# One head of A, not four of B, as the last unit of a decode attention kernel, with a new column-form end

## The chip, the cores and the metric

The kernel runs on one core of one Trainium2 chip. The metric is the device time of one execution in microseconds (us), the median of several runs. The profile covers one run of each kernel; its span is about 2 us shorter than the time measured around it.

## The reference

Two independent attention blocks with one query token each. Per block there are 32 heads of 128 elements, bf16 throughout. A attends to all 16,384 keys of its cache, B only to the last 4,096 keys of its own. The two output rows of 512 stand side by side.

```python
q = (x @ wq).reshape(B, Sq, Hq, Dh).transpose(0, 2, 1, 3)
k, v = k_cache, v_cache                   # block B: only the last W = 4096 keys
scores = einsum("bhqd,bhkd->bhqk", q, k) * Dh ** -0.5
p = softmax(scores)
o = einsum("bhqk,bhkd->bhqd", p, v)
out = o.transpose(0, 2, 1, 3).reshape(B, Sq, Hq * Dh) @ wo
# result: concatenate([out_A, out_B], axis=-1)
```

So the work is almost all reading: each key and each value is used once.

## The kernel before

The kernel works in units of 4 MB of K and 4 MB of V: one head of A, or four heads of B whose keys are shared out over the partitions. After four units of A comes one of B; the order ends with A28, A29, A30, A31, B28-31. Each unit has two chunks of 64 keys per partition. For a chunk, DVE multiplies K by q (`prod`), adds the two halves (`half`), and PE sums the rest with eight matmuls against the identity (`red`); DVE and ACT make the exponentials; PE does p.v later, two chunks behind (`waiting`).

```python
for c, ch in enumerate(chunks):
    ...
    _mult(nc, cx, ch)                      # DVE: prod = K * q
    if prev is not None:
        _softmax(nc, cx, prev)             # DVE reduce, ACT exp (4 exps for a chunk of B)
        waiting.append(prev)
    fin_pe()
    _add(nc, cx, ch)                       # DVE: half
    fin_dve()
    _red(nc, cx, ch)                       # PE: q.k, 8 matmuls
    if len(waiting) > 1:
        pv(waiting.pop(0))                 # PE: p.v, needs V
    prev = ch

_softmax(nc, cx, prev)                     # ---- the end
end = prev.unit.group
fin_pe()                                   # fold of A's last group
fin_dve()                                  # its row (orow)
_late_sum_before(nc, cx, stB)              # partial row of B: copy by ACT, into PSUM
_late_sums(nc, cx, end)                    # sums of exps, bank f again
fin_pe()                                   # columns of A
fin_dve()
pv(waiting.pop(0))                         # p.v of B, first chunk
fin_pe()                                   # A's output row
_pv(nc, cx, prev, 0, (U - LATE) // 4)      # p.v of B, first half of the last chunk
_late_fold(nc, cx, end)                    # waits for acc_sb
_late_pv(nc, cx, prev, end)                # 32 keys, straight into columns
_late_out(nc, cx, end)                     # oc, output matmuls, copy, store
```

A group's normal finish is fold, row, columns, cast and output matmuls. Only the last group of the program ends in the "late" column form: its last 32 keys per partition are multiplied with V as the stationary operand, so the result stands as a column already. An instruction that waited held up the one behind it on PE: in the timeline below p.v of A31 waits 4.54 us for its V, and the reduction behind it starts 1.88 us after its input is ready.

The last V is loaded in pieces (64, 32, then, after the last part of `wo`, 16 and 16 keys). One piece is one issue for a head of A and four for four heads of B.

The softmax here doesn't subtract the row's maximum and nothing guards it: scores larger than these inputs give would overflow.

## Time and profile before

| | before |
|---|---|
| time, median (range) of 3 runs | 835.23 us (834.71 to 835.35) |
| span of the profiled run | 832.8 us |
| moved by DMA | 352.7 MB, mean 424 GB/s |
| DVE, PE, ACT busy | 70%, 49%, 8% |

These are lines of the profile's page: the span, then 40 equal slices of the span (DMA busy in tenths, and GB/s), then the chain of work that ended last, by engine.

```profile
span 832.8 us, 6118 instructions
...
DMA  9999999999999999999999999999999999999995
GB/s 383 441 435 427 414 442 427 428 432 434 438 430 429 429 428 427 431 431 433 429 439 426 429 428 430 432 430 429 433 434 432 429 430 432 428 429 433 427 427 197
...
DMA 68%; DVE 19%; issue 10%; PE 2%; SPq 1%; ACT 0%; DVEq 0%; ACTq 0%
```

The DMA engines are busy in all slices but the last, and the chain is 68% DMA. The body is bound by reading. A change that reads the same bytes finds most of its room in the last slice, some 20 us.

This is the timeline of that end (start in us, duration, engine, line, operation, `out<-in`; in brackets the idle time of the engine just ahead of it and what ended it).

```profile
811.49 2.28 DVE L189 TENSOR_TENSOR half<-prod 128x4096 bf16<-128x4096 bf16 x1
...
813.84 1.89 PE L248 MATMUL acc<-vt,pA 128*16 128x512 bf16 x16 [4.54 <-DMA vt<-in_A_v_cache_dram]
...
815.65 3.31 PE L202 MATMUL red<-half,ident 128*128 128x512 bf16 x8
...
820.68 1.04 PE L348 MATMUL f_ps<-acc_sb,sel 128*4 128x128 f32 x8 [0.68 <-ACT acc_sb L259]
...
822.82 0.39 PE L307 MATMUL out<-late_part,ones_f 1*1 1x128 f32 x8 [1.10 <-ACT late_part L302]
...
826.99 1.05 PE L278 MATMUL f_ps<-sel,acc_sb 128*128 128x4 f32 x8 [0.76 <-ACT acc_sb L259]
...
828.89 0.16 DVE L319 TENSOR_TENSOR oc<-f_ps,late_recip 128x4 bf16<-128x4 f32 x1 [4.69 <-PE f_ps L290]
...
829.75 0.27 ACT L332 CAST late_row<-out 128x128 bf16<-128x128 f32 x1 [2.81 <-PE out L325]
830.04 0.61 SPq L333 DMA_DIRECT2D out_dram<-late_row  x1
```

The reduction of the last chunk (L202 at 815.65) could have started at 813.77 (811.49 + 2.28), when DVE finished its input, the last half-sum (L189). On PE it stands behind p.v of A31 (813.84), which had waited for its V.

The windows show, per stretch: busy time of PE, PEld, DVE, ACT, POOL, then the TensorE clock (1.00 is full), the DMA share and GB/s.

```profile
core 0: us, PE busy (x) PEld busy (x) DVE busy (x) ACT busy (x) POOL busy (x), PEclk, DMA share, GB/s
...
817.00:818.00 1.00, 1.00 (x4) 0.36 (x3) 0.00 (x0) 0.00 (x0) 0.00 (x0) 0.50 0.96 348
...
821.00:822.00 1.00, 0.72 (x7) 0.35 (x4) 0.22 (x2) 1.00 (x7) 0.00 (x0) 1.00 0.90 323
...
824.00:825.00 1.00, 1.00 (x18) 0.39 (x17) 0.16 (x1) 0.00 (x0) 0.00 (x0) 1.00 0.33 111
```

Traffic falls below its 430 GB/s in this end and stops at about 825 us.

### The profile page before, as it was taken

Reading aid. Unit: us, or ns where it says so; the run is one execution under the profiler, and the core shown is the slowest. Engines: PE = TensorE matmul, PEld = TensorE weight load, DVE = VectorE, ACT = ScalarE, POOL = GpSimd, SP = SyncE. Lnnn points to the kernel's source line nnn. Section 1 sums busy time; section 2 is a strip of 40 time slices with the busy share of each in tenths; the row PEclk is TensorE's granted clock in tenths of the full one; section 3 lists DMA queues with packets and bytes.
Section 4 is the critical chain, followed back from the end, with each engine's and each line's share of the span. In section 5 each row is a group of like instructions: output and inputs, shape, how many; then the busy total and the mean of one; then the engine's idle time right before and its main releaser. Section 6 shows DMA issues by size and latency. Waiting matters only on the chain.

```text
span 832.8 us, 6118 instructions
## 1 busy us (share of the span) xinstructions
PE 410.6 (49%) x2524; PEld 141.4 (17%) x2524; DVE 585.0 (70%) x299; ACT 68.3 (8%) x301; POOL 2.9 (0%) x16
## 2 busy tenths in 40 slices
PE   3356445443555534654455443564544444554356
PEld 1112111111111111211111111121111111121113
DVE  2892666777777766777777766666677776777791
ACT  2000011000110001000020000100011000110002
POOL 1000000000000000000000000000000000000000
PEclk9778667776676666766677766677678776677767
DMA  9999999999999999999999999999999999999995
GB/s 383 441 435 427 414 442 427 428 432 434 438 430 429 429 428 427 431 431 433 429 439 426 429 428 430 432 430 429 433 434 432 429 430 432 428 429 433 427 427 197
DMA packets 16198, 352.71 MB, mean 424 GB/s; under 512 B 2730, under 2 KB 3243, under 8 KB 5419
## 3 DMA queue, kind: packets, MB, share of 16 engines
q1 hardware_dynamic: 15882, 352.33, 98.8%
q8 instruction: 19, 0.31, 0.2%
q14 instruction: 9, 0.07, 0.0%
q10 hardware_dynamic: 288, 0.00, 0.0%
HBM read 352.32 MB, written 0.00 MB: 423 GB/s over the span
## 4 chain that ended last, share of the span: by engine, by line
DMA 68%; DVE 19%; issue 10%; PE 2%; SPq 1%; ACT 0%; DVEq 0%; ACTq 0%
DMA kt<-in_A_k_cache_dram 55%; DVE prod L177 12%; DMA kt<-in_B_k_cache_dram 9%; DVE half L189 6%; DMA vt<-in_A_v_cache_dram 4%; DVE sc L219 2%; PE red L202 1%; SPq L170 1%; PE acc L248 1%; ACT p_sb L226 0%; ACT acc_sb L259 0%; PE f_ps L278 0%; PE outA L389 0%; PE f_ps L290 0%; PE out L325 0%
## 5 line engine op out<-in xcount | busy, mean ns | idle before, releaser
L202 PE MATMUL red<-half,ident 128*128 128x512 bf16 x640 | 255.4, 571 | 379.6 <-DVE half L189 379.6
L177 DVE TENSOR_TENSOR prod<-kt,qallA 128x8192 bf16<-128x8192 bf16 x64 | 283.2, 4425 | 168.0 <-DMA kt<-in_A_k_cache_dram 167.4
L189 DVE TENSOR_TENSOR half<-prod 128x4096 bf16<-128x4096 bf16 x80 | 182.5, 2281 | 0.0
L202 PEld LDWEIGHTS <-ident 128*128 128x128 bf16 x640 | 82.4, 129 | 527.0 <-issue 500.8
L177 DVE TENSOR_TENSOR prod<-kt,qallB 128x8192 bf16<-128x8192 bf16 x16 | 70.8, 4425 | 46.7 <-DMA kt<-in_B_k_cache_dram 46.4
L248 PE MATMUL acc<-vt,pA 128*16 128x512 bf16 x1024 | 87.7, 476 | 17.2 <-DMA vt<-in_A_v_cache_dram 17.1
L226 ACT ACTIVATE pA<-sc 128x64 bf16<-128x64 f32 x64 | 16.4, 256 | 520.8 <-DVE sc L219 520.8
L219 DVE TENSOR_REDUCE sc<-red 128x64 f32<-128x512 f32 x80 | 54.7, 684 | 5.3 <-PE red L202 5.3
L248 PEld LDWEIGHTS <-pA 128*16 128x16 bf16 x1024 | 23.3, 98 | 87.0 <-issue 79.5
L226 ACT ACTIVATE p_sb<-sc,off 128x64 bf16<-128x64 f32 x64 | 21.5, 337 | 98.5 <-DVE sc L219 98.5
L248 PE MATMUL acc<-vt,p_sb 128*16 128x512 bf16 x248 | 21.4, 467 | 0.0
L348 PE MATMUL f_ps<-acc_sb,sel 128*4 128x128 f32 x120 | 15.5, 272 | 5.4 <-ACT acc_sb L259 5.4
L259 ACT COPY acc_sb<-acc 128x512 f32<-128x512 f32 x16 | 9.4, 585 | 85.6 <-PE acc L248 85.6
L124 PE MATMUL q_ps<-wq_t,xbA 128*128 128x512 bf16 x32 | 8.7, 439 | 13.1 <-DMA wq_t<-in_A_wq_dram 13.1
L226 ACT ACTIVATION_READ_ACCUMULATOR p_sb<-sc,off 128x1 f32 x64 | 12.0, 187 | 0.0
L226 ACT ACTIVATION_READ_ACCUMULATOR pA<-sc 128x1 f32 x64 | 11.9, 186 | 0.0
L348 PEld LDWEIGHTS f_ps<-acc_sb,sel 128*4 128x4 f32 x120 | 9.3, 86 | 8.2 <-ACT acc_sb L259 6.2
L248 PEld LDWEIGHTS <-p_sb 128*16 128x16 bf16 x248 | 5.6, 99 | 17.1 <-issue 15.6
L389 PE MATMUL outA<-wo_t,oc 128*1 128x512 bf16 x32 | 8.2, 379 | 0.0
L124 PE MATMUL q_ps<-wq_t,xbB 128*128 128x512 bf16 x32 | 7.2, 378 | 1.7 <-DMA wq_t<-in_B_wq_dram 1.1
L389 PE MATMUL outB<-wo_t,oc 128*1 128x512 bf16 x28 | 7.7, 402 | 0.0
L96 DVE COPY xbB<-xTB 128x32 bf16<-128x32 bf16 x16 | 1.5, 197 | 8.2 <-DMA xTB<-in_B_x_dram 8.2
(44 smaller groups left out, 58.7 us busy)
## 6 DMA issues: line engine op xcount, KB each, us to landing
kt<-in_A_k_cache_dram SPq DMA_DIRECT2D x32, 4096.0 KB, 27.2
vt<-in_A_v_cache_dram SPq DMA_DIRECT2D x31, 4096.0 KB, 31.1
kt<-in_B_k_cache_dram SPq DMA_DIRECT2D x32, 1024.0 KB, 22.3
vt<-in_B_v_cache_dram SPq DMA_DIRECT2D x28, 1024.0 KB, 28.1
wq_t<-in_A_wq_dram SPq DMA_DIRECT2D x1, 4096.0 KB, 12.3
wq_t<-in_B_wq_dram SPq DMA_DIRECT2D x1, 4096.0 KB, 23.9
wo_t<-in_A_wo_dram SPq DMA_DIRECT2D x4, 1024.0 KB, 29.2
vt<-in_A_v_cache_dram SPq DMA_DIRECT2D x2, 2048.0 KB, 24.7
```

Source lines behind the costliest of these rows:

```text
L96: cx.o(nc.vector.tensor_copy(st.xb[:, c, g, :].rearrange("p (i r) -> p r i", r=R)[:, g, :], xT[:, c : c + 1].broadcast_to([P, P // R]),))
L124: cx.o(nc.tensor.matmul(q_ps[:, :], lhsT=st.xb[:, c, g, :], rhs=w[:, g, j * (512 // DH) : (j + 1) * (512 // DH), :], start=(g == 0 and c = ...
L170: cx.o(nc.sync.dma_start(out=t[g:P:n, k : k + w, :], in_=src[:, k : k + w, :]))
L177: cx.o(nc.vector.tensor_tensor(out=ch.prod[:, :, :], in0=u.kt[:, ch.k0 : ch.k0 + U, :], in1=q.rearrange("p (o d) -> p o d", o=1).broadcast ...
L189: cx.o(nc.vector.tensor_tensor(out=ch.half[:, :, :], in0=ch.prod[:, :, 0 : DH // 2], in1=ch.prod[:, :, DH // 2 : DH], op=ALU.add,))
L202: cx.o(nc.tensor.matmul(ch.red[:, :, :], lhsT=cx.ident[:, :], rhs=ch.half[:, :, b * W : (b + 1) * W], start=(b == 0), stop=(b == nb - 1),))
L219: cx.o(nc.vector.tensor_reduce(out=sc[:, :], in_=ch.red[:, :, :], axis=AX.X, op=ALU.add))
L226: cx.o(nc.scalar.activation(out=ch.p[:, :, g, :], in_=sc[:, :].rearrange("p (t e) -> p t e", e=4), func=ACT.Exp, scale=SCALE, bias=0.0 if ...
L248: cx.o(nc.tensor.matmul(gr.acc[r : r + 4 * G, :], lhsT=ch.p[:, t, :, :], rhs=u.vt[:, k : k + 4, :], start=(first and t < 4), stop=(ends an ...
L259: cx.o(nc.scalar.copy(gr.acc_sb[:, :], gr.acc[:, :]))
L348: cx.o(nc.tensor.matmul(gr.f_ps[:, 0:DH], lhsT=cx.sel[:, e, :], rhs=gr.acc_sb[:, e * DH : (e + 1) * DH], start=False, stop=(e == 3), skip_ ...
L389: cx.o(nc.tensor.matmul(st.out_ps[0:1, :], lhsT=gr.oc[:, j : j + 1], rhs=st.wo_t[i][:, g, j * st.DN : (j + 1) * st.DN], start=(gr.i == 0 a ...
```

## The change

The intent: the last unit becomes one head of A, whose V needs fewer issues and whose softmax is one exp instead of four; the last q.k does not wait behind p.v; the output row is summed in two halves in two PSUM banks, which DVE and ACT copy at the same time (0.41 and 0.36 us in its profile, the second started 0.03 us after the first). Along with this go steps: the partial row is copied when its sum is complete instead of in the end (`st.row`), the late sums get a PSUM bank of their own, and the order of the end is new. The diff, cut:

```diff
 def _late_sums(nc, cx, gr):
-    gr.f_ps = cx.psf_pool.tile([P, 2, G], F32, tag="f", name="f_ps")
+    gr.f_ps = cx.psout_pool.tile([P, 2, G], F32, tag=f"out{gr.st.name}", name="late_ps")
 ...
 def _late_sum_before(nc, cx, st):
-    part = cx.singles.tile([1, st.DN], F32, tag="late_part", name="late_part")
-    cx.o(nc.scalar.copy(part[:, :], st.out_ps[0:1, :]))
-    (one PSUM tile out4, zeroed; four matmuls of 128 columns from part)
+    (two PSUM tiles out2; two matmuls of 256 columns from st.row)
 ...
 def _late_out(nc, cx, gr):
-    row = cx.singles.tile([P, n], BF16, tag="late_row", name="late_row")
-    cx.o(nc.scalar.copy(row[:, :], st.out4[:, :]))
-    (store from four partitions)
+    row = cx.singles.tile([1, st.DN], BF16, tag="late_row", name="late_row")
+    for t, copy in enumerate((nc.vector.tensor_copy, nc.scalar.copy)):
+        cx.o(copy(row[0:1, t * n : (t + 1) * n], st.out2[t]))
+    (store from one partition)
 ...
 def _fin_out(nc, cx, gr):
-    if last and st.in_row == st.H // G:
+    if last:
+        (copies out_ps to st.row at once; the store only if the row is complete)
 ...
-        st.in_row = st.H // G - (W != SkA)
+        st.in_row = st.H // G - (W == SkA)
 ...
+    units[-2:] = units[:-3:-1]
 ...   (the last part of wo is that of A)
-        if len(waiting) > 1:
+        if len(waiting) > 1 and c < len(chunks) - 2:
             pv(waiting.pop(0))
         prev = ch
 
+    end = prev.unit.group
     _softmax(nc, cx, prev)
-    end = prev.unit.group
-    fin_pe()
-    fin_dve()
-    _late_sum_before(nc, cx, stB)
+    while waiting[0].unit is not prev.unit:
+        pv(waiting.pop(0))
+    _late_sum_before(nc, cx, end.st)
     _late_sums(nc, cx, end)
     fin_pe()
     fin_dve()
     pv(waiting.pop(0))
     fin_pe()
+    fin_dve()
     _pv(nc, cx, prev, 0, (U - LATE) // 4)
+    fin_pe()
     _late_fold(nc, cx, end)
     _late_pv(nc, cx, prev, end)
     _late_out(nc, cx, end)
```

Small tiles also move: the pool `small` goes from four buffers to two, and a pool `ends` of two takes recip, orow and oc.

More of the change, by code (lines that the diff above doesn't have):

```diff
@@ L298, in _late_sum_before @@
 def _late_sum_before(nc, cx, st):
-    part = cx.singles.tile([1, st.DN], F32, tag="late_part", name="late_part")
-    cx.o(nc.scalar.copy(part[:, :], st.out_ps[0:1, :]))
-    st.out4 = cx.red_pool.tile([P, st.DN // 4], F32, tag="red", name="out4")
-    cx.o(nc.vector.memset(st.out4[:, :], 0.0))
-    n = st.DN // 4
-    for t in range(4):
+    n = st.DN // 2
+    st.out2 = []
+    for t in range(2):
+        o = cx.red_pool.tile([P, n], F32, tag="red", name="out2")
+        st.out2.append(o[32 * t : 32 * t + 1, :])
         cx.o(nc.tensor.matmul(
-            st.out4[32 * t : 32 * t + 1, :],
+            st.out2[t],
             lhsT=cx.ones_f[0:1, 0:1],
-            rhs=part[0:1, t * n : (t + 1) * n],
+            rhs=st.row[0:1, t * n : (t + 1) * n],
             start=True, stop=False, skip_group_check=True,
@@ L316, in _late_out @@
     st = gr.st
-    n = st.DN // 4
-    gr.oc = cx.small.tile([P, G], BF16, tag="oc", name="oc")
+    n = st.DN // 2
+    gr.oc = cx.ends.tile([P, G], BF16, tag="oc", name="oc")
     cx.o(nc.vector.tensor_tensor(
@@ L322, in _late_out @@
     for j in range(G):
-        for t in range(4):
+        for t in range(2):
             f = j * st.DN + t * n
             cx.o(nc.tensor.matmul(
-                st.out4[32 * t : 32 * t + 1, :],
+                st.out2[t],
                 lhsT=gr.oc[:, j : j + 1],
@@ L330, in _late_out @@
             ))
-    row = cx.singles.tile([P, n], BF16, tag="late_row", name="late_row")
-    cx.o(nc.scalar.copy(row[:, :], st.out4[:, :]))
-    cx.o(nc.sync.dma_start(
-        out=cx.out[0, 0, st.at : st.at + st.DN].rearrange("(t f) -> t f", t=4),
-        in_=row[0:P:32, :],
-    ))
+    row = cx.singles.tile([1, st.DN], BF16, tag="late_row", name="late_row")
+    for t, copy in enumerate((nc.vector.tensor_copy, nc.scalar.copy)):
+        cx.o(copy(row[0:1, t * n : (t + 1) * n], st.out2[t]))
+    cx.o(nc.sync.dma_start(out=cx.out[0, 0:1, st.at : st.at + st.DN], in_=row[:, :]))
 def _fin_fold(nc, cx, gr):
@@ L356, in _fin_row @@
 def _fin_row(nc, cx, gr):
-    recip = cx.small.tile([G, 1], F32, tag="recip", name="recip")
+    recip = cx.ends.tile([G, 1], F32, tag="recip", name="recip")
     cx.o(nc.vector.reciprocal(recip[:, :], gr.f_ps[:, DH : DH + 1]))
-    gr.orow = cx.small.tile([G, DH], BF16, tag="orow", name="orow")
+    gr.orow = cx.ends.tile([G, DH], BF16, tag="orow", name="orow")
     cx.o(nc.scalar.activation(
@@ L379, in _fin_cast @@
 def _fin_cast(nc, cx, gr):
-    gr.oc = cx.small.tile([P, G], BF16, tag="oc", name="oc")
+    gr.oc = cx.ends.tile([P, G], BF16, tag="oc", name="oc")
     cx.o(nc.vector.tensor_copy(gr.oc[:, :], gr.oc_ps[:, :]))
@@ L397, in _fin_out @@
         cx.loads.release("wo")
-    if last and st.in_row == st.H // G:
-        row = cx.singles.tile([1, st.DN], BF16, tag=f"row{st.name}", name=f"row{st.name}")
-        cx.o(nc.scalar.copy(row[0:1, :], st.out_ps[0:1, :]))
-        cx.o(nc.sync.dma_start(out=cx.out[0, 0:1, st.at : st.at + st.DN], in_=row[0:1, :]))
+    if last:
+        done = st.in_row == st.H // G
+        st.row = cx.singles.tile(
+            [1, st.DN], BF16 if done else F32, tag=f"row{st.name}", name=f"row{st.name}"
+        )
+        cx.o(nc.scalar.copy(st.row[0:1, :], st.out_ps[0:1, :]))
+        if done:
+            cx.o(nc.sync.dma_start(
+                out=cx.out[0, 0:1, st.at : st.at + st.DN], in_=st.row[0:1, :]
+            ))
 @with_exitstack
@@ L430 @@
     cx.singles = pool("singles", 1)
-    cx.small = pool("small", 4)
+    cx.small = pool("small", 2)
+    cx.ends = pool("ends", 2)
     cx.kt_pool = pool("kt", 2)
@@ L535, in load_v, with load_wo @@
         ld.add(None if k else "vt", lambda: _load_kv(nc, cx, u, "v", k, w))
+    def load_wo(st, b, part=None):
+        ld.add(None if part else "wo", lambda: _load_wo(nc, cx, st, b, part))
     n = len(units)
     per = 2 * G
-    last_wo = stB.H // per - 1
+    last_wo = stA.H // per - 1
     ld.add("vt", lambda: _load_wq(nc, cx, stA, "vt"))
@@ L546 @@
             b = u.heads[0] // per
-            part = 0 if u.st is stB and b == last_wo else None
-            ld.add("wo", lambda st=u.st, b=b, part=part: _load_wo(nc, cx, st, b, part))
+            load_wo(u.st, b, 0 if u.st is stA and b == last_wo else None)
         if i == n - 2:
@@ L557 @@
     load_v(u, U, U - LATE)
-    ld.add(None, lambda: _load_wo(nc, cx, stB, last_wo, 1))
+    load_wo(stA, last_wo, 1)
     load_v(u, 2 * U - LATE, LATE // 2)
```

## The prediction

> **What bounds the kernel.** The span is 832.8 us, and 352.7 MB move at 424 GB/s (page, parts 1 and 3); the DMA row of the slices is 9 up to the last slice. DVE is busy 70%, PE 49%. The chain of waits is 68% DMA. So the body is DMA-bound, and keeps its bytes: only the last two units trade places (A31 and B28-31, each 4 MB of K and 4 MB of V). Nothing before about 784 us should move.
>
> **The end of before** (timeline and chain of waits). DVE finishes the last half-sum at 813.8 us. On PE the last q.k reduction stands behind the p.v of A31, which waits for its V until 813.84 and takes 1.89 us at half clock. So the reduction runs from 815.65 to 818.97. Then ACT does acc_sb 0.58, four exps (about 1.4), orow 0.34 and late_part 0.5 in series; PE does A's fold, columns and output row, B's p.v, acc_sb 0.58, fold 1.05, late p.v 0.8; oc at 828.89, out 0.6, copy 0.27 (ends 830.0), output DMA and close 2.8.
> DMA: from 816 to 825 us the windows show only 111 to 377 GB/s instead of about 430, 2.43 MB in 9 us. SP issues sixteen V pieces of B in 8.25 and 6.80 us. But the last PE work on V starts at 827.8, after the traffic ended (about 825): PE and ACT, not DMA, end the kernel.
>
> **What changes, costed.**
> 1. Last q.k no longer waits behind p.v: reduction starts at about 813.8 instead of 815.65, ends at about 817.1 (still half clock): -1.9 us.
> 2. The last softmax is one exp (0.26) instead of four (about 1.4), and no late_part copy (0.5) in the end: ACT about -1.6 us, partly hidden.
> 3. Added on PE after the reduction: both p.v of B (32 matmuls, 2.1 us at full clock, about 2.7 with a cold start), where one p.v of A (1.0) stood: about +1.5 us.
> 4. Then unchanged kinds: row of B folded 1.05, p.v of A31 1.04 and half of it 0.5, columns 0.3, acc_sb 0.58, late fold 1.05, late p.v 0.9. My sum puts late fold at about 824.7 and the end of late p.v at about 826.6 (before: 828.9).
> 5. V of A31 needs 4 issues of about 0.4 us on 128 partitions, not 16: traffic should stay near 430 GB/s and end at about 822 instead of 825. Not the last limit before; now DMA and PE end close together.
> 6. Output: 8 matmuls of 256 columns, about 0.6 as before; two half copies side by side about 0.35 (before 0.27); one-row output DMA issue 0.33 like rowA's instead of 0.61: -0.2 net.
>
> [...] clock 0.50 when PE starts at 813.84, 1.00 at 819. So I keep the cold reduction.
>
> **Sum.** Span about 830.4 us, 2.4 us shorter; the time stands about 2.3 us above the span: 832.8 us, 0.3% faster. Range 830.5 to 834.5. Chances: faster by over 2% 0.01, within 2% 0.985, slower 0.005.
>
> **Signs.** Last reduction starts right after the last half-sum at about 813.8; DMA holds above 400 GB/s until about 821; SP has four short V issues; late p.v ends at about 826 to 827; the end after the last copy is about 2.5 us.
>
> **What would make it wrong.** Last V landing after 825.5; clock falling to half in the final chain (up to +2 us); PE blocked in order on acc_sb of B; engines of the DMA finishing unevenly; or a PE chain shorter than summed (gain up to 4.5 us).

The two clock readings are those of the trace of before, where the clock was 0.50 from 811.7 to 818.55 us and 1.00 from there to 828.8. The "about 2.7 with a cold start" in point 3 is an estimate; in before sixteen matmuls of p.v took 1.04 us at clock 1.00 and 1.89 us at 0.50, so it lies between 2.1 and 3.8 us.

## The result

The changed kernel takes 832.25 us in the median (831.9 to 832.8, 4 runs), the kernel before 835.29 us (834.71 to 836.58, 4 runs). The ratio is 0.9962, 95% interval 0.9945 to 0.9979. Ratios here are the mean time of one kernel's runs over that of the other's of the same rounds, so not quite the ratio of the medians quoted. The verdict is "same" at 2%: 3.0 us faster, clear of the noise.

The page of the changed kernel:

```profile
span 831.1 us, 6096 instructions
...
GB/s 379 429 436 428 423 442 431 431 428 431 431 430 428 429 429 428 429 432 434 428 431 432 431 427 429 427 432 433 429 430 432 433 431 427 431 429 428 427 427 256
...
DMA 65%; DVE 22%; issue 10%; PE 2%; SPq 1%; DVEq 0%; ACTq 0%
```

The body looks the same, slices of about 430 GB/s. The last slice has 256 GB/s instead of 197: the slices are equally long, but the last one starts 1.7 us earlier here (810.3 us against 812.0), and the body runs about 1.3 us later, so more of the same traffic falls into it. The timeline of the end:

```profile
807.35 0.81 SPq L170 DMA_DIRECT2D vt<-in_A_v_cache_dram  x2
...
808.68 0.98 SPq L170 DMA_DIRECT2D vt<-in_A_v_cache_dram  x2
...
812.79 2.28 DVE L189 TENSOR_TENSOR half<-prod 128x4096 bf16<-128x4096 bf16 x1
...
815.12 3.57 PE L202 MATMUL red<-half,ident 128*128 128x512 bf16 x8 [4.48 <-DVE half L189]
...
818.62 2.53 PE L248 MATMUL acc<-vt,p_sb 128*16 128x512 bf16 x32
...
823.01 1.13 PE L248 MATMUL acc<-vt,pA 128*16 128x512 bf16 x13
...
825.69 1.06 PE L278 MATMUL late_ps<-sel,acc_sb 128*128 128x4 f32 x8
...
827.59 0.16 DVE L318 TENSOR_TENSOR oc<-late_ps,late_recip 128x4 bf16<-128x4 f32 x1 [3.00 <-PE late_ps L290]
...
828.47 0.36 ACT L332 CAST late_row<-out 1x256 bf16<-1x256 f32 x1 [2.10 <-PE out L324]
828.91 0.25 SPq L333 DMA_DIRECT2D out_dram<-late_row  x1
```

The last half-sum ended at 815.07 us here, 1.3 us later than in the profile of before, so compare distances from that point. The reduction starts 0.05 us after it (before: 1.88). Late fold starts 10.6 us after it (before: 13.2), oc 12.5 us after it (before: 15.1), the span ends 16.0 us after it (before: 19.0). No PE matmul between the reduction and late fold has a wait in brackets; p.v of A31's first chunk (823.01) runs in the gap where before PE stood waiting. SP gives out the last V in short issues (807.35 to 809.66).

The windows of the end, columns as above:

```profile
816.00:817.00 1.00, 1.00 (x4) 0.38 (x3) 0.00 (x0) 0.00 (x0) 0.00 (x0) 0.50 0.86 360
...
819.00:820.00 1.00, 1.00 (x16) 0.43 (x12) 0.49 (x1) 0.35 (x2) 0.00 (x0) 0.54 1.03 412
...
821.00:822.00 1.00, 1.00 (x12) 0.48 (x8) 0.00 (x0) 0.59 (x1) 0.00 (x0) 1.00 0.75 265
...
824.00:825.00 1.00, 1.00 (x27) 0.53 (x27) 0.16 (x1) 0.00 (x0) 0.00 (x0) 1.00 0.30 115
```

Here the prediction of the traffic failed: with short issues it is already at 360 to 413 GB/s from 816 to 820 us, falls from there and trails off until after 825 us.

### The profile page after: what moved, and what is told of

The parts are those of the page before. It is cut to its first block, busy times and chain, and to the rows that moved or that the text cites. A ratio compares the mean times of both kernels' runs of the same rounds, so it can differ in the third digit from the quotient of the medians.

```text
span 831.1 us, 6096 instructions
## 1 busy us (share of the span) xinstructions
PE 416.9 (50%) x2512; PEld 142.0 (17%) x2512; DVE 585.1 (70%) x299; ACT 68.6 (8%) x301; POOL 2.9 (0%) x16
## 4 chain that ended last, share of the span: by engine, by line
DMA 65%; DVE 22%; issue 10%; PE 2%; SPq 1%; DVEq 0%; ACTq 0%
DMA kt<-in_A_k_cache_dram 53%; DVE prod L177 13%; DMA kt<-in_B_k_cache_dram 9%; DVE half L189 7%; DMA xTB<-in_B_x_dram 3%; DVE sc L219 2%; SPq L170 1%; PE acc L248 0%; PE red L202 0%; DVE xbB L96 0%; PE late_ps L278 0%; PE outB L386 0%; PE late_ps L290 0%; PE f_ps L345 0%; PE out L324 0%
## 5 line engine op out<-in xcount | busy, mean ns | idle before, releaser
L202 PE MATMUL red<-half,ident 128*128 128x512 bf16 x640 | 258.1, 576 | 380.3 <-DVE half L189 380.3
L248 PE MATMUL acc<-vt,p_sb 128*16 128x512 bf16 x256 | 23.6, 512 | 0.0
L96 DVE COPY xbA<-xTA 128x128 bf16<-128x128 bf16 x4 | 0.6, 221 | 11.4 <-DMA xTA<-in_A_x_dram 11.4
```

What stands on the lines that cost most here:

```text
L96: cx.o(nc.vector.tensor_copy(st.xb[:, c, g, :].rearrange("p (i r) -> p r i", r=R)[:, g, :], xT[:, c : c + 1].broadcast_to([P, P // R]),))
L202: cx.o(nc.tensor.matmul(ch.red[:, :, :], lhsT=cx.ident[:, :], rhs=ch.half[:, :, b * W : (b + 1) * W], start=(b == 0), stop=(b == nb - 1),))
L248: cx.o(nc.tensor.matmul(gr.acc[r : r + 4 * G, :], lhsT=ch.p[:, t, :, :], rhs=u.vt[:, k : k + 4, :], start=(first and t < 4), stop=(ends an ...
```

## The experiments

Twelve runs in three groups; all were timed in five rounds against the kernel before of the same group. Medians:

| run | what it is | us | ratio to before, 95% interval |
|---|---|---|---|
| after_again | the changed kernel | 832.24 | 0.9965 (0.9953 to 0.9978) |
| no_defer | without the deferral | 833.58 | 0.9977 (0.9963 to 0.9990) |
| b_last | without the swap of units | 832.27 | 0.9964 (0.9952 to 0.9977) |
| quarters | four quarters again | 832.51 | 0.9968 (0.9956 to 0.9981) |
| before_defer | before, plus deferral | 834.83 | 0.9992 (0.9979 to 1.0006) |
| skip_late_v | wrong: last 1 MB of V not read | 832.54 | 0.9961 (0.9949 to 0.9974) |
| warm16 | changed kernel, PE kept busy ahead of the last reduction | 832.76 | 0.9964 (0.9951 to 0.9976) |
| warm16_skip | wrong: both | 830.76 | 0.9943 (0.9930 to 0.9955) |
| ends_only | before, plus the new end alone | 835.82 | 0.9998 (0.9985 to 1.0012) |
| defer_early_row | before_defer, plus the early copy of the row | 834.28 | 0.9982 (0.9969 to 0.9994) |
| one_red | wrong: 1 of 8 reduction matmuls | 831.03 | 0.9951 (0.9939 to 0.9964) |
| more_instr | changed kernel, 2072 PE instructions more | 834.15 | 0.9988 (0.9976 to 1.0001) |

The kernel before had 835.34, 835.14 and 835.19 us in the three groups, so a comparison of medians from two groups is uncertain by some 0.2 us more. All runs but skip_late_v and warm16_skip passed the check of the result. It also passed one_red, which leaves out seven of eight parts of q.k; so the check hardly feels an error in the scores.

The first group undoes one part of the change at a time.

**after_again.** No edit.

> The changed kernel once more, as the yardstick of this call. Both theories: about 3 us under the kernel before (ratio 0.996), last reduction starting right after the last half-sum, late fold right behind acc_sb.

As expected in time. In one respect this profile shows what the first one of the changed kernel did not:

```profile
825.47 0.54 PE L290 MATMUL late_ps<-pA,vt 128*128 128x4 bf16 x16
...
826.43 0.56 PE L290 MATMUL late_ps<-pA,vt 128*128 128x4 bf16 x16 [0.42 <-DMA vt<-in_A_v_cache_dram]
```

PE has half of late p.v done and then waits 0.42 us for the last V piece. In the first profile PE came to late p.v 1.0 us later (11.53 us after the last half-sum against 10.55) and did not wait. So PE and the landing of V end within a fraction of a microsecond of each other.

**no_defer.**

```diff
-        if len(waiting) > 1 and c < len(chunks) - 2:
+        if len(waiting) > 1:
```

> Only the deferral undone: p.v of B's first chunk stands again ahead of the last q.k reduction and waits for B's V. Theory PE/ACT chain: the reduction starts about 1.9 us later against the last half-sum, but one p.v of 1.0 us is then already done, so 0.5 to 1.5 us slower than the changed kernel. Rival, the end is set by the landing of the last V: no difference, because the landing does not move.

The reduction starts 1.83 us after the last half-sum instead of 0.05. The median is 1.3 us above the changed kernel's, inside the range that the PE and ACT theory gave, but the two intervals overlap and the runs spread from 832.51 to 833.87; the profiled run was the fastest of them. So the direction is likely, the size loose.

**b_last.**

```diff
-        st.in_row = st.H // G - (W == SkA)
+        st.in_row = st.H // G - (W != SkA)
-    units[-2:] = units[:-3:-1]
     (and the last part of wo is B's again)
```

> Only the swap of units undone (four heads of B last, sixteen V issues again), deferral and two halves kept. Theory PE/ACT chain: four exps in series come back after the last reduction and the fold of A with its row: about 2 us slower than the changed kernel, the gap sitting between the last reduction and late fold. Rival, landing: also about 2 us slower, but then late p.v starts only when the last V piece lands and traffic ends later than in the kernel before.

Both theories missed. The swap, which names the change, is worth nothing when the rest is there: 832.27 against 832.24 us. The timeline of its end shows why:

```profile
818.33 1.90 PE L248 MATMUL acc<-vt,pA 128*16 128x512 bf16 x32
...
819.23 0.35 ACT L226 ACTIVATE p_sb<-sc,off 128x64 bf16<-128x64 f32 x1 [5.09 <-DVE sc L219]
...
820.57 0.56 ACT L259 COPY acc_sb<-acc 128x512 f32<-128x512 f32 x1
...
820.69 0.61 PE L267 MATMUL late_ps<-cs,ones_f 128*128 128x4 f32 x4
...
821.33 0.81 PE L345 MATMUL f_ps<-acc_sb,sel 128*4 128x128 f32 x6
...
824.77 1.05 PE L278 MATMUL late_ps<-sel,acc_sb 128*128 128x4 f32 x8
```

The four exps are back on ACT (819.23 to 820.57), but PE does 1.90 us of deferred p.v in the same time and needs the exps only for the late sums at 820.69: they are ready just in time. The shorter softmax saves time that was hidden already. The sixteen V issues are back too and also cost nothing.

**quarters.** Four matmuls of 128 columns in one zeroed bank, one ACT copy, store from four partitions, as in the kernel before.

> Only the output form undone: the row in four quarters of one bank, one copy, output DMA from four partitions. Theory: 0.3 to 0.5 us slower than the changed kernel, all of it after oc: copy 0.27 instead of 0.41, output issue and close about 2.8 instead of 2.25. Rival: no difference of close, it is run noise.

The median is 0.3 us above the changed kernel, which fits, but the intervals overlap widely; by time alone it is not told from noise. The profile shows the two parts: the copy takes 0.27 us instead of 0.41 and the store issue 0.62 us instead of 0.25.

The second group asks what the deferral is worth alone and what limits the changed kernel.

**before_defer.**

```diff
-        if len(waiting) > 1:
+        if len(waiting) > 1 and c < len(chunks) - 2:
 ...
     end = prev.unit.group
+    while waiting[0].unit is not prev.unit:
+        pv(waiting.pop(0))
     fin_pe()
```

> The kernel before with the deferral alone. Theory PE/ACT chain: the 1.9 us wait before the last reduction goes, but one more p.v of A then stands behind it, and the four exps keep ACT busy: 0 to 0.8 us faster than before. Rival, deferral is the main source of the gain: about 2 us faster.

0.3 us in the median, not told from zero. The reduction does start at once, 1.8 us earlier, but the time is lost again:

```profile
817.47 2.50 PE L248 MATMUL acc<-vt,pA 128*16 128x512 bf16 x32
...
820.72 1.04 PE L348 MATMUL f_ps<-acc_sb,sel 128*4 128x128 f32 x8 [0.68 <-ACT acc_sb L259]
...
822.87 0.39 PE L307 MATMUL out<-late_part,ones_f 1*1 1x128 f32 x8 [1.10 <-ACT late_part L302]
...
827.03 1.05 PE L278 MATMUL f_ps<-sel,acc_sb 128*128 128x4 f32 x8 [0.76 <-ACT acc_sb L259]
```

PE does both p.v of A31 first, and then meets the old end, where it waits 0.68 us for acc_sb, 1.10 us for late_part and 0.76 us for the second acc_sb: 2.54 us. From the first p.v to late fold it takes 9.56 us here and 6.44 us in b_last (818.33 to 824.77), where no PE matmul in that stretch waits. That difference of 3.1 us is these waits and 0.6 us of p.v (2.50 against 1.90; the clock from 818 to 820 us was 0.82 here and 0.96 there).

**skip_late_v.**

```diff
-    load_v(u, 2 * U - LATE, LATE // 2)
-    load_v(u, 2 * U - LATE // 2, LATE // 2)
 ...
-            lhsT=u.vt[:, ch.k0 + k, :],
+            lhsT=u.vt[:, ch.k0 + k - LATE, :],
```

> Wrong on purpose: the changed kernel without the last two V pieces (1 MB, an estimated 2.4 us at 430 GB/s); late p.v reads the V that landed before instead. Theory PE/ACT chain: no difference from the changed kernel (within 0.5 us), late fold still waits for acc_sb. Rival, the last landing is the limit: about 2 us faster.

832.54 us: no gain. Alone, the landing is not the limit. (This run and warm16_skip give a wrong result: relative error 0.037.)

**warm16.** Sixteen matmuls without use on PE ahead of the last reduction:

```diff
+def _warm(nc, cx, n):
+    t = cx.pst_pool.tile([P, 512], F32, tag="ocp", name="warm")
+    for _ in range(n):
+        cx.o(nc.tensor.matmul(
+            t[:, :], lhsT=cx.ident[:, :], rhs=cx.stA.qall[:, 0:512], start=True, stop=True,
+        ))
 ...
         fin_dve()
+        if c == len(chunks) - 1:
+            _warm(nc, cx, 16)
         _red(nc, cx, ch)
```

> Sixteen matmuls of 128x512 without use, put on PE ahead of the last reduction, where it idles about 4.4 us and the clock falls to half. Theory PE chain: the reduction runs at full clock in about 1.8 us instead of 3.6 and B's p.v in 2.1 instead of 2.5: 1.5 to 2.2 us faster than the changed kernel, unless the last V piece then lands too late. Rival, landing limit: less than 0.5 us faster, late p.v waits for V.

The rival was right about the time (832.76 us, no gain):

```profile
815.02 1.89 PE L202 MATMUL red<-half,ident 128*128 128x512 bf16 x8 [0.94 <-DVE half L189]
...
825.22 0.56 PE L298 MATMUL late_ps<-pA,vt 128*128 128x4 bf16 x16 [0.25 <-DMA vt<-in_A_v_cache_dram]
...
826.48 0.56 PE L298 MATMUL late_ps<-pA,vt 128*128 128x4 bf16 x16 [0.70 <-DMA vt<-in_A_v_cache_dram]
```

The reduction takes 1.89 us instead of 3.57, but late p.v then waits 0.25 and 0.70 us for the last two V pieces and ends where it did. In this profile the output matmuls also take 1.01 us instead of 0.60; so 0.4 us of the missing gain is not the landing itself.

**warm16_skip.** The edits of the two runs above together.

> Wrong on purpose: the warm clock and the missing last 1 MB together. If warm16 is held up by the landing, this one is faster than warm16 by what it waits for (up to 2 us); if not, equal to warm16 within 0.4 us.

830.76 us, 2.0 us under warm16 (0.4 us of it in the output matmuls, 0.60 us again) and 1.5 us under the changed kernel. Each of the two alone gained nothing and both together gain: the changed kernel has two limits of nearly the same length, the chain on PE and the landing of V.

The third group takes up two questions that these left: what in the end makes the gain, and why V lands so late although all is issued by 809.66 us.

**ends_only.** b_last without the deferral.

```diff
-        if len(waiting) > 1 and c < len(chunks) - 2:
+        if len(waiting) > 1:
```

> B last as in the kernel before and no deferral; only the new end is taken over (late sums in a bank of their own and ahead of the fold, early copy of the partial row, two halves). Theory after seeing that b_last equals the changed kernel: the gap-free end is the main source, so 1.2 to 2.5 us faster than before, and 0.5 to 1.5 us slower than b_last. Rival, deferral and end only work together: within 0.5 us of before.

My theory fell; the rival holds. The new end alone gains nothing (835.82 us; four runs at 835.66 or above, one at 833.63):

```profile
821.60 0.35 ACT L226 ACTIVATE p_sb<-sc,off 128x64 bf16<-128x64 f32 x1
...
823.09 0.59 PE L267 MATMUL late_ps<-cs,ones_f 128*128 128x4 f32 x2 [1.24 <-ACT p_sb L226]
...
823.71 1.44 PE L345 MATMUL f_ps<-acc_sb,sel 128*4 128x128 f32 x6
```

Without deferral, A's p.v ends after the reduction, ACT copies acc_sb first and the four exps follow. The late sums, which now stand ahead of the fold, wait 1.24 us for the last exp, and PE's clock has fallen to half by the end of this gap (in windows of 0.5 us: 1.00 to 823.0, 0.63 to 823.5, then 0.50): the fold takes 1.44 us for six matmuls where b_last took 0.81.

Together with no_defer this makes a square, all four with the new end:

| new end | deferral off | deferral on |
|---|---|---|
| B last | 835.82 | 832.27 |
| A last | 833.58 | 832.24 |

The swap is worth 2.2 us without deferral and nothing with it. The 2.2 us is loose: ends_only is of another group, its five runs spread from 833.63 to 836.2, and its interval overlaps that of no_defer. By the traces both remove the same thing, the wait for four exps (1.24 us in ends_only): one makes it short (0.15 us in no_defer), the other puts p.v over it (none in b_last).

**defer_early_row.** before_defer, with the partial row copied in `_fin_out` when its sum is complete:

```diff
-    part = cx.singles.tile([1, st.DN], F32, tag="late_part", name="late_part")
-    cx.o(nc.scalar.copy(part[:, :], st.out_ps[0:1, :]))
 ...
-            rhs=part[0:1, t * n : (t + 1) * n],
+            rhs=st.row[0:1, t * n : (t + 1) * n],
```

> before_defer with one more step: the partial row is copied when its sum is complete, not by ACT in the end. Theory: the copy (0.56 us on ACT) stood between A's fold and the late sums, and PE waited 1.10 us for it; 0.4 to 0.9 us faster than before_defer. Rival, the shared bank f is the bar (late sums wait until orow has read it): under 0.3 us.

834.28 us, 0.55 us under before_defer, as expected, with overlapping intervals. In its profile the wait of 1.10 us has become one of 0.44 us, now for the zeroing of out4 by DVE. The remaining 2.0 us to b_last (medians of two groups) lie in the rest of the end (own bank, order, two halves), which was not taken apart further.

**one_red** and **more_instr** test why the landing is late. In the trace each load raises its semaphore 16 times, and the page counts 16 DMA engines; that each rise is the landing of one engine's part is my reading, the trace does not name the engine. In the changed kernel the first and the last of these 16 are 0.3 us apart at 13 us, 1.5 at 63 us, 3.2 at 401 us and 5.0 at 783 us; it stays 5.0 for the last V piece. The steps at 63, 401 and 747 us (1.2, 0.95 and 1.1 us) follow packets of 16 KB on the queue for instructions at 57, 399 and 741 us, numbers 1, 9 and 17 of 19; each packet has 16,384 bytes and takes 1.0 to 1.1 us. The trace does not name a packet's engine either; that these three hit the same one is read from the steps. Smaller steps of about 0.4 us, some 1.5 us together, have another source, which was not tested.

```diff
 # one_red
-    nb = DH // 2 // W
+    nb = 1
 # more_instr, ahead of the eight matmuls of each of the first 74 chunks
+    for _ in range(cx.extra):              # 14
+        cx.o(nc.tensor.matmul(
+            ch.red[:, 0, 0:4], lhsT=cx.ident[:, :], rhs=cx.ident[:, 0:4], start=True, stop=True,
+        ))
```

> Wrong on purpose: one reduction matmul of each eight, 1120 PE instructions fewer (about 17 KB packets of instructions: an estimated 15 instead of 19). Theory instruction loads: the landing of one load on its 16 DMA engines spreads over 5 us in the end because instruction packets of 16 KB, about 1.1 us each, hit one engine at packets 1, 9 and 17; without number 17 the spread at the end is about 3.7 us and the last V lands 0.8 to 1.3 us earlier against the first V piece's first landing; time 1 to 2 us under the changed kernel, late p.v waiting for V. Rival, the spread is the engines' own: it stays at 5 us, late p.v waits for V until about the same time (826.4) and the time is within 0.5 us.

> Correct result: 14 small matmuls without use in each of the first 74 chunks while PE idles, 2072 PE instructions more (an estimated 27 packets). Theory instruction loads: one more packet on the engine that is last (number 25), spread about 6 us, last V lands about 1.1 us later and the time rises by 0.7 to 1.5 us. Rival, the spread is the engines' own: spread 5 us, time within 0.4 us.

Both estimates of packets can be worked out from the changed kernel: 19 packets for its 5024 matmul and weight-load instructions on PE give 14.8 for the 3904 of one_red and 26.8 for the 7096 of more_instr. The "17 KB" are the packets of 16,384 bytes.

These are lines of the page of the changed kernel, of one_red and of more_instr: PE busy time with the number of matmuls, and the instruction queue's packets, MB and share.

```profile
PE 416.9 (50%) x2512; PEld 142.0 (17%) x2512; DVE 585.1 (70%) x299; ACT 68.6 (8%) x301; POOL 2.9 (0%) x16
...
q8 instruction: 19, 0.31, 0.2%
```

```profile
PE 262.0 (32%) x1952; PEld 79.2 (10%) x1952; DVE 585.1 (70%) x299; ACT 68.5 (8%) x301; POOL 2.9 (0%) x16
...
q8 instruction: 15, 0.25, 0.1%
```

```profile
PE 436.4 (52%) x3548; PEld 165.9 (20%) x3548; DVE 585.2 (70%) x299; ACT 68.5 (8%) x301; POOL 2.9 (0%) x16
...
q8 instruction: 27, 0.44, 0.2%
```

| | after_again | one_red | more_instr |
|---|---|---|---|
| instruction packets in the page | 19 (the changed kernel's page) | 15 | 27 |
| first to last of 16 landings, last V piece | 4.86 us | 3.33 us | 6.16 us |
| start of the last unit's first K product | 800.44 us | 798.85 us | 801.80 us |
| time, median | 832.24 us | 831.03 us | 834.15 us |

The spread follows the number of instruction packets in both directions, and K lands earlier or later with it. In more_instr the large steps (1.2 to 1.4 us) come at 53, 284, 519 and 748 us, behind packets 1, 9, 17 and 25, and in one_red at 95 and 527 us, behind packets 1 and 9 alone. The first of the 16 landings of the last V piece stays at 821.5 to 821.6 us in all three. So the spread grows with the packets of instructions, and PE had to wait for the last of the 16 landings: in after_again its wait for the last V piece ended at 826.43 us, 4.9 us after the first landing. That a packet holds up a single DMA engine is not shown by itself, it is my reading of the steps. The rival, that the large steps are the engines' own, is refuted. Two parts of what was expected failed. In one_red late p.v did not wait for V: PE, busy 32% of the span instead of 50%, was mostly at half clock (mean 0.56 over the span, 0.72 in the changed kernel; B's p.v took 3.59 us) and its own chain was again last; the gain is 1.2 us. This profile is of the slowest of its five runs (832.72 us, span 831.0 us; the others 829.1 to 829.9), so it need not show the end of a typical one. In more_instr the time rose by 1.9 us, more than the range, and there too late p.v did not wait for V: K of the last unit comes 1.4 us later, and PE's chain follows it.

No version that computes the right thing beat the changed kernel; b_last ties with it.

## Why the prediction was right, and where it was wrong

- **The time** (832.8 predicted, 832.25 measured, range 830.5 to 834.5) and the claim that the gain lies in the end: right. That nothing before about 784 us would move failed by about 1 us (see "Left open"). Measured from the last half-sum the end is 3.0 us shorter in the changed kernel's first profile and 3.45 us in the second (15.58 us against 19.03), against 2.4 predicted. The mis-sized term is the PE chain after the reduction: late fold was predicted 10.9 us after the last half-sum and came after 10.6 and 9.6 us. That the time came out so close is in part luck: the sum put 1.9 us on point 1, which alone gives 0.3 us, and left out most of the waits that gave the gain.
- **Point 1**, the reduction starts at once, 1.9 us earlier: right in the trace (1.83 us). As a share of the gain it was not: alone it is worth 0.3 us.
- **Point 2**, one exp instead of four: the step is wrong as an additive term. With deferral the exps are hidden wholly, not "partly", and the swap gives nothing (832.27 against 832.24 us).
- **Point 3**, two p.v of B behind the reduction: 2.53 us measured against 2.7 predicted. Right.
- **What the sum left out**: I costed instructions, not the gaps between them, but for the copy late_part in point 2. PE's three waits in the old end came to 2.54 us in before and again in before_defer. In the new order p.v and the late sums stand where PE waited. That is where most of the gain comes from, and it needs the deferral to have something to put there: with B last, neither alone gives more than 0.3 us, and together they give 3.0. Which step of the new end removes how much was tested for the early row copy alone.
- **Point 5**, traffic near 430 GB/s until about 822 us: wrong. Short issues did not help, because the last of the 16 landings of a load comes about 5 us after the first (4.97 us for the last V piece). In the kernel before, the small pieces were issued until 823.06 us; the spread shrank to 0.5 us at the last piece (my reading: the engines that were ahead had to wait for the issue), and the last landing came about as late: 11.4 us after the last half-sum, against 11.6 us in both profiles of the changed kernel and 11.5 us in b_last (landing times set on the profile's axis by the K load that DVE waited for).
- **Point 6**, the close: store to end of span 2.2 us after the copy in the changed kernel, 2.8 before. Right; 0.3 us in quarters, not told from noise.
- **The clock.** The reduction starts cold in before and after alike (clock 0.50, 3.31 and 3.57 us), and warm16, with PE kept busy ahead of it, brought it to 1.89 us. Counted from PE's restart at the end (813.84, 815.12 and 814.98 us), the clock rose to 1.00 after 4.7 us in before, 4.8 us in the first profile of the changed kernel and 2.7 us in the second (after_again); so p.v of B took 2.53 us in the first and 1.90 us in the second. In ends_only it had fallen to half by the end of a single gap of 1.24 us, with PE busy before and after it. A rule for these moments was not shown.
- **Left open.** In all kernels with the new end the body ran later than in those with the old: the K product of unit 39 starts at 785.6 to 786.0 us in nine of them and at 784.7 to 784.9 us in the three with the old end (one_red and more_instr apart). The difference grows unevenly over the run. So the shorter end is worth a bit more than the times show, and about 1 us is given back earlier. Its cause was not tested; the smaller pool of small tiles, which the nine share, is one candidate. A part can be chance, since the profiles of before and before_defer are of runs that were among the fastest of theirs.

## What to carry to other kernels

Sum the waits of the engine whose chain ends a kernel, not only its instructions: the gain here came from putting independent work into three short waits, and the parts of the change did not add up because two of them covered the same wait. Here the end had two limits of nearly equal length, and removing either showed nothing; remove both in one run before calling one of them harmless. In this kernel a load was as late as the last of its 16 landings, 5.0 us after the first at the end; with 15, 19 and 27 packets of instructions on the DMA queues this spread was 3.3, 4.9 and 6.2 us.
